# G, U and the turned state in a chunked state recurrence on one Trainium2 core: two column halves on TensorE, all copies on ScalarE

## The chip, the cores and the metric

The kernel runs on one core of one Trainium2 chip. The metric is the device time of one execution in microseconds. Before the change it was timed three times: the median is 735.41 us (730.02 to 738.67). Five engines work side by side, each through its own queue in program order: TensorE (PE, with its weight loads shown apart as PEld), VectorE (DVE), ScalarE (ACT), GpSimd (POOL) and SyncE (SP), which issues the DMAs.

## The reference

The inputs are r, k, v, w, a, b of shape 4 x 8 x 768 x 40 (32 heads, 768 steps, 40 features). A recurrence over the steps makes the output of each head, and a small mixture of four attention experts then reads it:

```
for t in range(S):
    y[:, :, t] = np.einsum('bhd,bhde->bhe', rt, state)
    Sa = np.einsum('bhde,bhe->bhd', state, at)
    state_decay = state * wt[:, :, None, :] - np.einsum('bhd,bhe->bhde', Sa, bt)
    state = state_decay + np.einsum('bhd,bhe->bhde', vt, kt)
...
for e in range(E):
    scores = scale * (q @ k.transpose(0, 2, 1))      # causal
    ye = softmax(scores) @ v @ wo[e]
    out += gate of the top 2 of 4 experts * ye
```

The change touches the recurrence alone.

## The kernel before, in words

The 768 steps are cut into 24 chunks of 32 steps (index c), and four chunks make one of six rounds (w). The 32 heads are cut into four groups of eight (g). A **unit** u = 4c + g is one chunk for eight heads, so there are 96 units, and 16 of them make a round. For a unit the kernel runs seven short stages, each a burst of TensorE products into PSUM with a copy behind it:

- s_k (L358) transposes keys and b's; two ScalarE copies (L365) put them into LS.
- s_g (L366) makes G: for each of eight heads one product with 33 stationary columns and 40 moving columns (L371) into one PSUM tile `ps`, then one ScalarE copy of 32 x 320 (L372) into GT.
- s_u (L373) makes U from G by the inverted triangle in TT (L377), then one ScalarE copy of 32 x 320 with the sign turned (L378) into R2.
- s_v (L379) transposes V and U (L383), copied by ScalarE (L384) into VU.
- s_f (L385) makes the masked products (L388); VectorE applies the mask (L389).
- s_y (L390) makes the outputs and the new state (L396) from LS and R2. Even heads go to PSUM partitions 0 to 39 and odd heads to 64 to 103, by `tile_position=(0, 64 * s)`. ScalarE copies the state out (L406), or VectorE scales it in the last chunk of a round (L404). The function that s_y returns (`decay`, L408) has VectorE scale the outputs.
- s_t (L415) runs for every second unit: it transposes the new state of 16 heads into the PSUM tile `pt` (L420) and copies it, "turned", into the next chunk's LS in two pieces of 40 x 320. For g = 0 the copies are ScalarE's (L427), for g = 2 VectorE's (L425).

A loop over iterations n writes the stages of different units in the fixed order of the table MAIN (L433): u of unit n-1, g of unit n, y of unit n-3, f of unit n-2, t of unit n-6 (n even), a k now and then, and v of unit n-1. So y at iteration n+1 needs the turned state that t copied at iteration n.

Between the stages the table SIDE (L30; SIDE1 and SIDE2 for the first rounds) places the preparation of later rounds by iteration and by slot, a slot being the place behind the stage of that number in MAIN. Preparation means scans over the decays (L267, L273), products with them (L276, L281) and mask copies (L290) on VectorE, 16 matmuls at a time (L289) on TensorE, flags (L264) and copies (L283) on ScalarE. The inversion of the next round's triangles is a chain of two-operation steps (L319, L321) split between POOL and VectorE; its result goes through memory by DMA (L323, L326) into TT. Slot 3, which takes most of VectorE's side work, lies between the mask of f (L389, with L408) and the copies of t (L425).

The products of s_k, s_g, s_u, s_v, s_f and L289 share four PSUM buffers `ps` in turn (L151); `py` has two, `pt` one. After the 96 units comes the attention part (from L650), which the change leaves as it was.

Of the kernel before, what the change touches and what calls it, by code (L numbers as in the profile page):

```python
# [8 lines left out]
AF = mybir.ActivationFunctionType  # L9
# [132 lines left out]
def recurrence(tc, ctx, I, xT, FL, CM, early, tail=None, KP=(11, 11, 11, 11, 11, 11)):  # L142
# [5 lines left out]
    V, A, T, PL = nc.vector, nc.scalar, nc.tensor, nc.gpsimd  # L148

    def ps(shape):  # L150
        return pp.tile(shape, F32, name="ps", tag="ps", bufs=4)  # L151
# [41 lines left out]
    hd = lambda t, d: t.rearrange("p (h d) -> p h d", d=d)  # L193
# [156 lines left out]
    def unit(u):  # L350
        c, g = divmod(u, 4)
        w, cw = divmod(c, 4)
        i = w * NG + g
        h0 = 8 * g
        gl, tt, ls, r1, r2, rb, sc = GF[w % 2], TF[w % 2], LS[c % 2], R1[c % 2], R2[c % 2], RB[c % 2], SC[i % 12]
        gt, vu, xt, py = GT[g], VU[u % 2], XT[g // 2][:, 4 * (g % 2):4 * (g % 2) + 4], PY[u % 2]
        rn, ln = R1[(c + 1) % 2], LS[(c + 1) % 2]
        def s_k():  # L358
            p_k = ps([128, 4, 128])
            for p in range(4):  # L360
                T.transpose(p_k[:, p, 0:104], KB[i % NKB][0:104, p * 4 + cw:p * 4 + cw + 2, :].rearrange("q c k -> q (c k)"),  # L361
                            ident[0:104, 0:104])
            p_k = p_k.rearrange("q p (s e) -> q (p s) e", s=2)[:, :, 0:40]
            for k in range(2):
                A.activation((ls, ln)[k][0:64, h0:h0 + 8], p_k[64 * k:64 * k + 64], AF.Copy)  # L365
        def s_g():  # L366
            p_g = ps([33, 8, 40])
            for h in range(8):
                o = 1024 * g + 64 * ((h // 2) * 4 + cw) + 32 * (h % 2)
                r = 104 * ((h0 + h) // 2) + 64 * (h % 2)  # L370
                T.matmul(p_g[:, h], gl[:, o:o + 33], r1[:, r:r + 40], start=True, stop=True)  # L371
            A.activation(gt[32 * g:32 * g + 32], p_g[0:32], AF.Copy)  # L372
        def s_u():  # L373
            p_u = ps([33, 8, 40])
            for h in range(8):
                o = 64 * ((h // 2) * 4 + cw) + 32 * (h % 2)
                T.matmul(p_u[:, h], tt[:, o:o + 33], gt[:, h, :], start=True, stop=True)  # L377
            A.activation(hd(r2[32:64, 40 * h0:40 * h0 + 320], 40), p_u[0:32], AF.Copy, scale=-1.0)  # L378
        def s_v():  # L379
            p_t = ps([80, 4, 66])  # L380
            for p in range(4):
                o = 40 * (h0 + 2 * p)
                T.transpose(p_t[:, p], r2[0:66, o:o + 80], ident[0:66, 0:66])  # L383
            A.activation(vu[0:80], p_t[:, :, 0:64], AF.Copy)  # L384
        def s_f():  # L385
            p_f = ps([64, 8, 32])
            for p in range(4):
                T.matmul(p_f[:, 2 * p:2 * p + 2], vu[:, p, :], rb[:, 4 * g + p, :], start=True, stop=True)  # L388
            V.tensor_tensor(hd(r2[0:64, 1280 + 32 * h0:1536 + 32 * h0], 32), p_f, mask[:, None, :].to_broadcast([64, 8, 32]), op=OP.mult)  # L389
        def s_y():  # L390
            a = r2[:, 0:40]
            for p in range(4):
                for s in range(2):
                    h = h0 + 2 * p + s
                    m = bass.AP(a.tensor, a.offset + 40 * h, [a.ap[0], [1280 - 8 * h, 2], [1, 40]])
                    T.matmul(py[64 * s:64 * s + 40, p], ls[:, h, :], m, start=True, stop=True, tile_position=(0, 64 * s))  # L396
            for s in range(2):
                q = slice(64 * s, 64 * s + 40)
                if c < 23:
                    o = rn[64:104, 52 * h0:52 * h0 + 416].rearrange("q (p e) -> q p e", p=4)[:, :, 64 * s:64 * s + 40]  # L400
                    st = py[q, :, 0]
                    if cw == 3:
                        pn = PC[((c + 1) // 4 * NG + g) % 12]
                        V.tensor_tensor(o, st, pn[q, :, None].to_broadcast([40, 4, 40]), op=OP.mult)  # L404
                    else:
                        A.activation(o, st, AF.Copy)  # L406
            def decay():
                V.tensor_tensor(xt[:, :, 32 * cw:32 * cw + 32], py[0:104, :, 1, 0:32],  # L408
                                sc.rearrange("q (p c) t -> q p c t", p=4)[:, :, cw, 0:32], op=OP.mult)
                if cw == 3:  # L410
                    for s in range(2):
                        nc.sync.dma_start(xT.rearrange("b (p s e) t -> b s e p t", s=2, e=40)[g, s, :, :, 128 * w:128 * w + 128],
                                          xt[64 * s:64 * s + 40])
            return decay
        def s_t():  # L415
            if c == 23:
                return
            for P in range(8):
                o = 52 * h0 + 104 * P
                T.transpose(PT[0:104, P // 4, 104 * (P % 4):104 * (P % 4) + 104], rn[0:104, o:o + 104], ident[0:104, 0:104])  # L420
            for s in range(2):
                o = ln[64:104, h0 + s:h0 + 16:2].rearrange("q (b p) e -> q b p e", b=2)
                x = PT[64 * s:64 * s + 40, :, 0:416].rearrange("q b (p e) -> q b p e", p=4)[:, :, :, 64:104]
                if g:
                    V.tensor_copy(o, x)  # L425
                else:
                    A.activation(o, x, AF.Copy)  # L427
        return dict(k=s_k, g=s_g, u=s_u, v=s_v, f=s_f, y=s_y, t=s_t)


# [80 lines left out]
    for n in range(NU + 4):  # L511
# [4 lines left out]
        for s, (x, d) in enumerate(MAIN):  # L516
            if x == "k":
                g = {7: 0, 1: 1, 3: 2, 5: 3}.get(n % 8)
# [440 lines left out]
```

## Time and profile before

| what | value |
|---|---|
| median of three runs | 735.41 us |
| profiled execution, its own time | 737.55 us |
| its span | 735.5 us |
| PE, PEld busy | 636.8, 563.0 us |
| DVE, ACT, POOL busy | 519.7, 466.6, 333.5 us |
| the units (first L371 to last L396) | 69.7 to 482.9 us |
| matmul instructions of G, U and y in the trace | 1536 each |

Busy time is the time in which an engine has at least one instruction running. For PE it says little on how much faster it could go, because matmuls overlap. "PEclk" is the clock that TensorE was granted, as a share of the full one. A wait is idle time of an engine put down to the instruction whose end released it; idle time of an engine that nobody waits for costs nothing. Each product of a head shows as two matmul instructions, so the eight of a stage are 16.

### The profile page before, as it was taken

To read this page: it belongs to the slowest core of one execution; us is meant where nothing else is said; L and a number is where in the kernel's file an instruction comes from. 1 tells how busy PE (TensorE), PEld (TensorE's weight loads), DVE (VectorE), ACT (ScalarE), POOL (GpSimd) and SP (SyncE) were. 2 spreads that over 40 slices of the span, in tenths; PEclk is the share of its full clock that TensorE was granted. 3 is DMA by queue.
4 is the path that set the end of the run, shared out by engine and by line. 5 is a ranking of instruction groups with operands and counts; after the bars stand their busy time and mean duration, and the time that the engine had idled before them with its cause. 6 is when DMAs were issued, how large, how long until landed. Compare 5 with 4: busy or idle time off the path is not lost.

```text
span 735.5 us, 22110 instructions
## 1 busy us (share of the span) xinstructions
PE 636.8 (87%) x8801; PEld 563.0 (77%) x8801; DVE 519.7 (71%) x1270; ACT 466.6 (63%) x1144; POOL 333.5 (45%) x512
## 2 busy tenths in 40 slices
PE   5531798898899888988899999979989999999996
PEld 4531788897789777987798999978868777887774
DVE  8899879668866876677657435258797687658651
ACT  6695487477657755766566768727656565656752
POOL 5475388139704850486018301013565354433641
PEclk8555799999999989989999999999999999999999
DMA  7851653575357535753452382143123113201101
GB/s 201 201 149 37 133 159 107 121 199 137 97 136 190 129 89 124 199 130 96 112 147 70 96 227 72 34 140 98 44 69 96 36 39 86 62 28 45 37 32 45
DMA packets 88551, 78.13 MB, mean 106 GB/s; under 512 B 54776, under 2 KB 72952, under 8 KB 88440
## 3 DMA queue, kind: packets, MB, share of 16 engines
q1 hardware_dynamic: 88296, 76.54, 39.9%
q8 instruction: 71, 1.16, 0.7%
q14 instruction: 40, 0.33, 0.2%
q10 hardware_dynamic: 144, 0.10, 0.1%
HBM read 56.17 MB, written 14.16 MB: 96 GB/s over the span
## 4 chain that ended last, share of the span: by engine, by line
PE 59%; DVE 22%; ACT 8%; issue 3%; DMA 1%; SPq 0%; POOL 0%; ACTq 0%; DVEq 0%; POOLq 0%
PE py L396 7%; PE ps L377 6%; PE ot L843 5%; PE ps L289 5%; PE ps L371 5%; PE ps L388 5%; PE sc L795 4%; PE pt L420 4%; PE pt L825 3%; PE pt L852 3%; PE pt L717 3%; PE ps L361 3%; PE pt L736 3%; DVE SC L273 2%; DVE MT L321 2%
## 5 line engine op out<-in xcount | busy, mean ns | idle before, releaser
L817 POOL TENSOR_TENSOR P<-P,m 128x128 f32<-128x128 f32 (+2 forms) x96 | 87.6, 934 | 103.1 <-DVE m L813 50.3
L396 PE MATMUL py<-R,LS 128*40 128x80 f32 x1536 | 84.9, 244 | 31.2 <-DVE LS L425 28.8
L289 PE MATMUL ps<-AB,KB 104*64 104x64 f32 x768 | 68.4, 262 | 38.6 <-ACT LS L365 16.1
L321 POOL TENSOR_TENSOR MT<-MT,TP 128x84 f32<-128x84 f32 (+13 forms) x169 | 89.9, 532 | 13.2
L289 PEld LDWEIGHTS ps<-AB,KB 104*64 104x64 f32 x768 | 63.3, 174 | 42.5 <-ACT LS L365 16.3
L389 DVE TENSOR_TENSOR R<-ps,CM 64x256 f32<-64x256 f32 x96 | 39.9, 415 | 78.4 <-PE ps L388 77.3
L396 PEld LDWEIGHTS py<-R,LS 128*40 128x40 f32 x1536 | 63.7, 122 | 36.3 <-DVE LS L425 33.8
L806 ACT ACTIVATE P<-sc,m 128x128 f32<-128x128 f32 (+2 forms) x96 | 60.7, 633 | 30.2 <-DVE m L805 24.5
L805 DVE TENSOR_REDUCE m<-sc 128x1 f32<-128x128 f32 (+2 forms) x96 | 59.4, 622 | 27.9 <-PE sc L798 26.8
L377 PE MATMUL ps<-GT,TT 128*33 128x40 f32 x1536 | 76.1, 207 | 0.0
L406 ACT ACTIVATE R<-py 40x160 f32<-40x160 f32 x144 | 42.5, 295 | 46.0 <-PE py L396 42.3
L377 PEld LDWEIGHTS ps<-GT,TT 128*33 128x33 f32 x1536 | 65.0, 116 | 7.5 <-issue 1.0
L795 PE MATMUL sc<-ks,qs 128*128 128x384 f32 (+4 forms) x256 | 64.4, 353 | 3.9 <-ACT P L806 3.6
L388 PE MATMUL ps<-RB,VU 128*64 128x64 f32 x768 | 63.4, 228 | 2.1 <-ACT VU L384 2.1
L365 ACT ACTIVATE LS<-ps 64x320 f32<-64x320 f32 x96 | 41.4, 431 | 30.6 <-PE ps L361 29.4
L388 PEld LDWEIGHTS ps<-RB,VU 128*64 128x64 f32 x768 | 56.1, 144 | 3.5 <-ACT VU L384 3.5
L825 PE MATMUL pt<-CM,P 128*128 128x128 f32 x336 | 51.9, 276 | 2.1 <-ACT pt L831 1.7
L319 POOL TENSOR_TENSOR TP<-LT,MT 128x220 f32<-128x220 f32 (+9 forms) x100 | 49.7, 497 | 7.8
L384 ACT ACTIVATE VU<-ps 80x256 f32<-80x256 f32 x96 | 36.4, 379 | 26.3 <-PE ps L383 24.5
L372 ACT ACTIVATE GT<-ps 32x320 f32<-32x320 f32 x96 | 40.7, 424 | 14.8 <-PE ps L371 11.4
L795 PEld LDWEIGHTS sc<-ks,qs 128*128 128x128 f32 x256 | 41.3, 191 | 11.2 <-ACT P L806 8.5
L378 ACT ACTIVATE R<-ps 32x320 f32<-32x320 f32 x96 | 40.9, 426 | 7.6 <-PE ps L377 5.6
(148 smaller groups left out, 1498.0 us busy)
## 6 DMA issues: line engine op xcount, KB each, us to landing
RB<-in_RB SPq DMA_DIRECT2D x24, 320.0 KB
EK<-in_EK SPq DMA_DIRECT2D x18, 416.0 KB
ks<-ks SPq DMA_DIRECT2D x32, 192.0 KB
R<-in_VG SPq DMA_DIRECT2D x24, 208.0 KB
EW<-in_EA SPq DMA_DIRECT2D x18, 214.5 KB
R<-in_VT SPq DMA_DIRECT2D x48, 80.0 KB
R<-in_RT SPq DMA_DIRECT2D x24, 160.0 KB
xT<-XT SPq DMA_DIRECT2D x48, 80.0 KB
```

What stands on the lines that cost most here:

```text
L289: T.matmul(p_a[:, p, cc, :], kb[0:104, n, :], AB[0:104, n, :], start=True, stop=True)
L319: return [lambda: e.tensor_tensor(tmp, row[:, None, :].to_broadcast([128, m, n]), M[:, r0:r0 + m, j][:, :, None].to_broadcast([128, m, n]) ...
L321: lambda: e.tensor_tensor(o, o, tmp, op=OP.add)]
L377: T.matmul(p_u[:, h], tt[:, o:o + 33], gt[:, h, :], start=True, stop=True)
L388: T.matmul(p_f[:, 2 * p:2 * p + 2], vu[:, p, :], rb[:, 4 * g + p, :], start=True, stop=True)
L396: T.matmul(py[64 * s:64 * s + 40, p], ls[:, h, :], m, start=True, stop=True, tile_position=(0, 64 * s))
L406: A.activation(o, st, AF.Copy)
L795: T.matmul(ps[:, c, 0:cw], QS[b][:, e, o], KS[b][:, e, z, k], start=(z == 0), stop=(z == 1 and not last), skip_group_check=True)
L805: V.tensor_reduce(m[:, 0, t:t + 1], ps[:, 0:ch, 0:cw], axis=AX.XY, op=OP.max, negate=True)
L806: later(DE, lambda: A.activation(pv, ps[:, 0:ch, 0:cw], AF.Exp, bias=m[:, 0, t:t + 1], accum_out=m[:, 1, t:t + 1]))
L817: PL.tensor_tensor(P[:, 0:n], P[:, 0:n], m[:, 3, t:t + 1].to_broadcast([128, n]), op=OP.mult)
L825: T.transpose(p[:, 128 * y:128 * y + 128], st["P"][t][:, 128 * c:128 * c + 128], ident)
```

## The change

G and U get PSUM tiles of 97 partitions and four columns of heads. The even heads are made in the array's columns from 0 and land on partitions 0 to 32, the odd heads in the columns from 64 and land on partitions 64 to 96, as y's heads already do. Each of the two copies of a unit becomes two pieces of 32 x 160, one for the even heads and one for the odd, and writes every second head. Both pieces of both copies of the turned state are ScalarE's.

```
         def s_g():
-            p_g = ps([33, 8, 40])
+            p_g = ps([97, 4, 40])
             for h in range(8):
-                o = 1024 * g + 64 * ((h // 2) * 4 + cw) + 32 * (h % 2)
-                r = 104 * ((h0 + h) // 2) + 64 * (h % 2)
-                T.matmul(p_g[:, h], gl[:, o:o + 33], r1[:, r:r + 40], start=True, stop=True)
-            A.activation(gt[32 * g:32 * g + 32], p_g[0:32], AF.Copy)
+                p, s = divmod(h, 2)
+                o = 1024 * g + 64 * (p * 4 + cw) + 32 * s
+                r = 104 * (h0 // 2 + p) + 64 * s
+                T.matmul(p_g[64 * s:64 * s + 33, p], gl[:, o:o + 33], r1[:, r:r + 40], start=True, stop=True, tile_position=(0, 64 * s))
+            for s in range(2):
+                A.activation(gt[32 * g:32 * g + 32, s::2], p_g[64 * s:64 * s + 32], AF.Copy)
         def s_u():
-            p_u = ps([33, 8, 40])
+            p_u = ps([97, 4, 40])
             for h in range(8):
-                o = 64 * ((h // 2) * 4 + cw) + 32 * (h % 2)
-                T.matmul(p_u[:, h], tt[:, o:o + 33], gt[:, h, :], start=True, stop=True)
-            A.activation(hd(r2[32:64, 40 * h0:40 * h0 + 320], 40), p_u[0:32], AF.Copy, scale=-1.0)
+                p, s = divmod(h, 2)
+                o = 64 * (p * 4 + cw) + 32 * s
+                T.matmul(p_u[64 * s:64 * s + 33, p], tt[:, o:o + 33], gt[:, h, :], start=True, stop=True, tile_position=(0, 64 * s))
+            for s in range(2):
+                A.activation(hd(r2[32:64, 40 * h0:40 * h0 + 320], 40)[:, s::2], p_u[64 * s:64 * s + 32], AF.Copy, scale=-1.0)
...
-                if g:
-                    V.tensor_copy(o, x)
-                else:
-                    A.activation(o, x, AF.Copy)
+                A.activation(o, x, AF.Copy)
```

The line numbers below the change move: L371 becomes L372, L372 becomes L374, L377 becomes L380, L378 becomes L382, L383 L387, L384 L388, L388 L392, L389 L393, L396 L400, L406 L410, L408 L412, and L425 and L427 both become L428.

VectorE's queue, in an iteration in which a round's side work stands between the mask of f and the turned state, before:

```order
L389 TENSOR_TENSOR R_127<-ps,CM 64x256
L408 TENSOR_TENSOR XT_132<-py_79,SC_94 104x4x32
L321 TENSOR_TENSOR MT_117<-MT_117,TP_119 128x7x13
L319 TENSOR_TENSOR TP_119<-MT_117 128x96
L321 TENSOR_TENSOR MT_117<-MT_117,TP_119 128x8x12
L273 SCALAR_TENSOR_TENSOR SC_99<-EW_83,D1P_86 104x528
L276 TENSOR_TENSOR AB_112<-EA_84,SC_99 40x16x32
L425 COPY LS_123<-pt 40x8x40 x2
L319 TENSOR_TENSOR TP_119<-MT_117 128x99
```

and now:

```order
L393 TENSOR_TENSOR R_127<-ps,CM 64x256
L412 TENSOR_TENSOR XT_132<-py_79,SC_94 104x4x32
L321 TENSOR_TENSOR MT_117<-MT_117,TP_119 128x7x13
L319 TENSOR_TENSOR TP_119<-MT_117 128x96
L321 TENSOR_TENSOR MT_117<-MT_117,TP_119 128x8x12
L273 SCALAR_TENSOR_TENSOR SC_99<-EW_83,D1P_86 104x528
L276 TENSOR_TENSOR AB_112<-EA_84,SC_99 40x16x32
L319 TENSOR_TENSOR TP_119<-MT_117 128x99
```

The pair of copies has left the queue, and nothing else in it has moved: the mask of the next f now follows the side work directly.

ScalarE's queue at such a place, before (an iteration and a half, from a flag on; VU is the copy of v, R_126 and R_127 that of u, GT that of g, py that of y):

```order
L264 ACTIVATE JK,FL<-EW_83,CM 104x512
L384 ACTIVATE VU_128<-ps 80x256
L378 ACTIVATE R_126<-ps 32x320
L372 ACTIVATE GT_134<-ps 32x320
L406 ACTIVATE R_125<-py_79 40x4x40 x2
L384 ACTIVATE VU_129<-ps 80x256
L378 ACTIVATE R_127<-ps 32x320
L372 ACTIVATE GT_135<-ps 32x320
```

and now:

```order
L264 ACTIVATE JK,FL<-EW_83,CM 104x512
L388 ACTIVATE VU_128<-ps 80x256
L382 ACTIVATE R_126<-ps 32x4x40 x2
L374 ACTIVATE GT_134<-ps 32x4x40 x2
L410 ACTIVATE R_125<-py_79 40x4x40 x2
L428 ACTIVATE LS_122<-pt 40x8x40 x2
L388 ACTIVATE VU_129<-ps 80x256
L382 ACTIVATE R_127<-ps 32x4x40 x2
L374 ACTIVATE GT_135<-ps 32x4x40 x2
```

The two copies of the turned state now stand between the copies of y and the copy of v, and the copies of u and g are two instructions each.

TensorE's queue keeps its order, but the other tile shape changes what its instructions wait for. Before:

```order
L361 MATMUL ps<-CM,KB_107 128x104 x3
L383 MATMUL ps<-CM,R_126 80x66 [waits DMAHW3_49,Activation_49]
L383 MATMUL ps<-CM,R_126 80x66 x3
L377 MATMUL ps<-GT_135,TT_120 33x40 [waits Activation_49]
L377 MATMUL ps<-GT_135,TT_120 33x40 x7
L371 MATMUL ps<-R_124,GLe 33x40 [waits DVE_49]
```

and now:

```order
L361 MATMUL ps<-CM,KB_107 128x104 x3
L387 MATMUL ps<-CM,R_126 80x66 [waits DMAHW3_49,PE_49,Activation_49]
L387 MATMUL ps<-CM,R_126 80x66 x3
L380 MATMUL ps<-GT_135,TT_120 33x40 [waits PE_49,Activation_49]
L380 MATMUL ps<-GT_135,TT_120 33x40 x7
L372 MATMUL ps<-R_124,GLe 33x40 [waits DVE_49]
```

Many products now wait for an earlier product of TensorE itself as well, the one that used the same `ps` buffer before. Counted over the whole queue, instructions with more than one wait carry 171 more of these further waits than before (586 against 415).

## Prediction, made before the changed kernel was run

> **What bounds the kernel now.** I read the page first, then the waits between 60 and 484 us (where the units run), then the busy time round by round, and at last the timeline at one of the long waits.
>
> ```profile
> span 735.5 us, 22110 instructions
> PE 636.8 (87%) x8801; PEld 563.0 (77%) x8801; DVE 519.7 (71%) x1270; ACT 466.6 (63%) x1144; POOL 333.5 (45%) x512
> PEclk8555799999999989989999999999999999999999
> PE 59%; DVE 22%; ACT 8%; issue 3%; DMA 1%; SPq 0%; POOL 0%; ACTq 0%; DVEq 0%; POOLq 0%
> ```
>
> TensorE leads with 87%, yet 22% of the chain that ended last is VectorE's. So there are places where PE stands and DVE sets the pace. The waits name them:
>
> ```profile
> engine line waited for: us in total, times, longest us
> PEld py L396 <- DVE LS L425: 33.8, 29, 3.4
> DVE XT L408 <- ACT R L406: 6.4, 13, 0.9
> PE py L396 <- DVE R L389: 2.2, 2, 1.6
> PE ps L388 <- ACT VU L384: 2.1, 8, 0.5
> ```
>
> Nearly all that PE waits for in steady work is one thing: y (L396) waits for VectorE's copies of the turned state, 29 times, 33.8 us. ScalarE's copies of the same kind (L427) release nobody there, and ScalarE as a whole holds PE up for little (2.1 us for VU). One such wait:
>
> ```profile
> 332.35 0.46 DVE L321 TENSOR_TENSOR MT<-MT,TP 128x96 f32<-128x96 f32 x1
> 332.72 0.41 ACT L372 ACTIVATE GT<-ps 32x320 f32<-32x320 f32 x1
> 332.74 1.25 DVE L273 TENSOR_TENSOR_SCAN SC<-EW,D1P 104x528 f32<-104x528 f32 x1
> 334.02 0.77 DVE L276 TENSOR_TENSOR AB<-EA,SC 40x512 f32<-40x512 f32 x1
> 334.82 1.01 DVE L425 COPY LS<-pt 40x320 f32<-40x320 f32 x2
> 335.36 0.33 PE L396 MATMUL py<-R,LS 128*40 128x80 f32 x2 [2.91 <-DVE LS L425]
> 336.67 0.62 ACT L406 ACTIVATE R<-py 40x160 f32<-40x160 f32 x2 [3.54 <-PE py L396]
> ```
>
> DVE works off its side jobs in order and reaches the copies late. ACT has been idle for 3.54 us meanwhile. By rounds of 16 units and the two stages behind them (first the stretch and its length, then the busy times in the header's order, then the granted clock):
>
> ```profile
> core 0: us, PE busy (x) PEld busy (x) DVE busy (x) ACT busy (x) POOL busy (x), PEclk, DMA share, GB/s
> 81.40:152.60 71.20, 63.60 (x1147) 59.17 (x1146) 54.91 (x118) 47.33 (x121) 36.22 (x63) 0.93 0.51 126
> 152.60:225.10 72.50, 63.97 (x1185) 59.42 (x1184) 56.18 (x124) 47.65 (x121) 37.71 (x64) 0.95 0.56 142
> 225.10:300.20 75.10, 66.54 (x1189) 61.84 (x1188) 55.45 (x123) 47.89 (x121) 36.74 (x64) 0.91 0.53 135
> 300.20:375.30 75.10, 66.78 (x1187) 62.33 (x1186) 52.78 (x120) 46.23 (x117) 37.07 (x64) 0.91 0.49 125
> 375.30:429.00 53.70, 51.88 (x1061) 48.90 (x1059) 30.21 (x85) 37.43 (x97) 25.56 (x61) 1.00 0.46 115
> 429.00:484.00 55.00, 53.11 (x1082) 49.84 (x1080) 21.15 (x57) 38.15 (x97) 3.97 (x12) 1.00 0.35 101
> ```
>
> Rounds 2 to 4 lose twice: PE idles some 8.5 us in each, and the granted clock falls to 0.91-0.95 on average, where it is 1.00 in the two stages without stalls. The last round splits into a heavy stretch of ten iterations and a light one:
>
> ```profile
> 309.60:359.30 49.70, 41.38 (x694) 38.17 (x692) 38.35 (x88) 29.42 (x79) 32.10 (x57) 0.86 0.41 112
> 359.30:378.30 19.00, 19.00 (x366) 18.06 (x363) 10.59 (x23) 12.10 (x27) 0.00 (x0) 1.00 0.59 121
> ```
>
> In the heavy one PE is idle for 8.3 us and runs at 0.86; in the light one it is busy throughout and sets the pace.
>
> **The change part by part: ScalarE and VectorE.**
>
> ```profile
> L425 DVE COPY LS<-pt x46: 483/490/496, 112.4 to 480.2; 40x320 f32<-40x320 f32 x46
> L427 ACT ACTIVATE LS<-pt x46: 428/430/433, 102.8 to 474.7; 40x320 f32<-40x320 f32 x46
> L372 ACT ACTIVATE GT<-ps x96: 411/425/428, 71.0 to 476.0; 32x320 f32<-32x320 f32 x96
> L378 ACT ACTIVATE R<-ps x96: 426/426/429, 82.9 to 477.8; 32x320 f32<-32x320 f32 x96
> L406 ACT ACTIVATE R<-py 40x160 f32<-40x160 f32 x144 | 42.5, 295 | 46.0 <-PE py L396 42.3
> ```
>
> DVE loses 46 x 0.49 = 22.5 us. ACT gains 46 x 0.43 = 19.8 us. A piece of 32 x 160 has the free size of L406's 295 ns, so two take 0.59 where one took 0.425: 0.165 us more, 192 times, 31.7 us. ACT goes from 466.6 to about 518 us, all of it before 484 us. Per unit it is 0.33 us, plus 0.86 for each pair of turned copies that moves. ACT has room for it: in the rounds it goes from some 47 to 47 + 5.3 + 4 = 56 of 75 us. Where that cover is gone, the 51.5 us lie on the path in part; that is the third rival.
>
> **TensorE.** The trace shows no product of 40 columns in halves. The nearest rows are of the undisturbed stage, at full clock:
>
> ```profile
> 413.06 0.69 PE ps L377 x16
> 413.75 0.54 PE ps L371 x15
> 414.29 0.59 PE py L396 x16
> 414.88 0.47 PE ps L388 x8
> ```
>
> An instruction with 40 columns in one half (L371) takes 0.54/15 = 36 ns and one with 64 columns (L388) 59 ns: 0.9 ns a column. L396 has 80 columns, but alternates between the two halves, and takes 0.59/16 = 37 ns: 0.46 a column, so the halves do overlap. If 40 columns follow that, a stage of 16 falls from 0.57 to 0.29 us. If 37 ns is instead what an instruction with its weight load needs, nothing is gained. Per unit (two stages) that is 0 to 0.57 us; lacking a row between, I take the middle, 0.28, or 27 us of PE time in 96 units. It counts only where PE sets the pace.
>
> The Trainium skill, page "TensorEngine Tiling (Array Packing)", section "Performance Considerations", speaks against this: each matmul has about 60 cycles of overhead, and no tiling factor should be taken from a dimension that is already small; 40 is below 60. By that G and U would stay as they are. The rows above differ in part, as 40 columns cost less than 64 in proportion.
>
> **The added waits.** TensorE has 171 further waits on itself, for products several bursts back, so they are met when reached. A further wait is an instruction of its own:
>
> ```profile
> L371 PEldq EVENT_SEMAPHORE  x43: 51/51/1749, 64.4 to 471.0; - x43
> ```
>
> At 51 ns that is 8.7 us if none is hidden by running ahead, 0 if all are. Such waits stand in L371's queue today and no wait row is put down to them, so I take nearer the lower end, 2.5. Behind a waiting one stands all of PE's queue.
>
> **The sum.** In the heavy stretch PE's work at full clock is 41.38 less the 0.14 x 49.7 = 7.0 that the half clock cost, 34.4 us, and 10 x 0.28 less in halves: 31.6. DVE's is 38.35 - 6 x 0.49 = 35.4. ACT's is 29.42 + 10 x 0.33 + 6 x 0.43 = 35.3. y no longer waits for side jobs that stand behind the mask of its own unit; DVE then has about an iteration to work them off. The floor is 35.4. In 375-429 us the span is 3.5% above the busiest engine, but there one engine leads alone; with three side by side I take 15%, 41 us, 8.7 less than now. The ends are 36.6 (3.5%) and 46.8 (only the copies' own 2.9 go). The other six iterations of a round gain 6 x 0.28 = 1.7 on a full PE (0 to 3.4). That is 10 a round; round 2 has less half clock, so 29 for rounds 2 to 4 (9 to 48). Round 1 idles partly for its start and has few of these copies: 5 (0 to 10). In 375-429 PE could give 1.8 idle and 16 x 0.28 = 4.5; I take 3.5 (-2 to 9). In 429-484 PE falls to 48.6 and ACT rises to 38.15 + 5.3 + 4.3 = 47.7, so they hinder each other: 2 (-4 to 6). After 484 us nothing changes. Together 29 + 5 + 3.5 + 2 - 2.5 = 37 us off the profiled execution's 737.55: 700.5. The median of the runs lies 2.1 below that execution: **698 us**.
>
> **The rivals.** First, the halves give nothing on short products (the skill's rule above): without 0.28 a unit the six light iterations and the last two stages gain about 10 less, and 709 follows. For it: 36 and 37 ns an instruction look alike. Against it: the cost per column. 12%.
>
> Second, VectorE stays the bound: y waits for the mask (L389) in the place of L425, since DVE has 35.4 us in the heavy stretch anyway. Then only 2.9 go there, three rounds give 3 x 4.4 = 13, round 1 gives 2, the rest 3: 18 off, 717. For it: DVE's 38.35 of 49.70 us with bursts. Against it: only 2.2 us of such waits today. 14%.
>
> Third, ScalarE becomes the bound and the time rises. The turned copies queue behind y's, u's and g's pieces, and now y waits for ACT at all 46 unit pairs and not at 29, at today's mean 33.8/29 = 1.17 us: 46 x 1.17 = 53.8 for 33.8, 20 us more; less some 8 of the halves it is 12 slower, 748. It decides from the point where ACT's work in an iteration passes PE's. For it: 47.7 against 48.6 in the last stage, and L408 of DVE already waits 13 times for L406. Against it: ACT's idle 3.54 us just where y waits. 8%. The same page of the Trainium skill, under "PSUM Bottleneck", advises both ScalarE and VectorE for emptying PSUM once tiling speeds up TensorE; the change does the opposite. ACT's 63% does not yet bear that out.
>
> Fourth, the three engines interlock well and the heavy stretches take 36.6 us: three rounds give 3 x (13.1 + 1.7) = 44, round 1 gives 8, the last stages 6 and 4; less 2.5 that is 59.5 off, 676. For it: all three have under 36 us of work there. Against it: bursts of 3 us (L273, L276, L425 above) have to even out within an iteration. 9%.
>
> **How the numbers follow.** The forecast has 57%. A measurement can tell about 1% (7 us) from no change. The range 674 to 722 leaves out the third rival and the outer edges of the second and the fourth. Faster by over 1% takes the forecast, the first, most of the second and the fourth: 0.86. Within 1%: 0.07, slower: 0.07.
>
> **What would show it.** Right: no wait of y for DVE's turned copies, waits of y below 12 us in all, PEclk near 1.00 in the rounds, L380 and L372 at 0.36-0.50 us for 16, pieces at 295 ns, rounds 2 to 4 at 62-66 us. Wrong: y waiting for L428 (ACT) or L393 (DVE) for more than 15 us, ACT busy above 90% in a round, or rounds above 70 us.

## The result, and the profile after

The changed kernel takes 697.9 us (median of 4 runs, 695.64 to 699.67); the kernel before, with one more run beside it, 736.95 us. The ratio is 0.9485, with a 95% interval of 0.9415 to 0.9555. The forecast was 698 us, range 674 to 722. The profiled execution took 697.25 us, its span is 695.5 us.

The page of the changed kernel, the lines that answer to those shown of before:

```profile
PE 591.6 (85%) x8801; PEld 503.5 (72%) x8801; DVE 498.6 (72%) x1224; ACT 521.2 (75%) x1382; POOL 338.2 (49%) x512
PEclk8555589999999999999999999999999999999998
PE 47%; DVE 20%; ACT 18%; issue 5%; DMA 4%; SPq 0%; POOL 0%; DVEq 0%; ACTq 0%; POOLq 0%
```

TensorE has lost 45 us of busy time (636.8 before), VectorE 21, and ScalarE has gained 55. The chain that ended last tells more than the sums: ScalarE's share of it has gone from 8% to 18% and TensorE's from 59% to 47%, while VectorE's is nearly what it was. The waits between 60 and 484 us, as far as y and the next buffers are concerned:

```profile
DVE XT L412 <- ACT R L410: 29.7, 42, 1.6
PEld ps L392 <- ACT VU L388: 12.5, 26, 1.3
PEld py L400 <- ACT LS L428: 9.7, 27, 0.8
PEld ps L372 <- ACT LS L365: 9.2, 9, 1.2
PEld ps L372 <- ACT R L410: 3.9, 11, 0.8
PEld ps L380 <- ACT GT L374: 3.2, 10, 0.4
PEld py L400 <- DVE R L393: 1.9, 2, 1.2
```

No row has y waiting for a turned copy of VectorE's any more; there were 33.8 us of it, the longest 3.4. In their place stand many short waits, and of the rows shown all but the last name ScalarE. The costs of the pieces and what TensorE's weight loads of y sat idle for, from the groups by line and form (busy us, mean ns of one, then the idle time before):

```profile
L400 PEld LDWEIGHTS py<-R,LS 128*40 128x40 f32 x1536 | 63.0, 119 | 15.0 <-ACT LS L428 9.7 <-DVE R L393 1.9 <-ACT VU L388 1.0
L382 ACT ACTIVATE R<-ps 32x160 f32<-32x160 f32 x192 | 56.7, 295 | 4.5 <-PE ps L380 1.2
L374 ACT ACTIVATE GT<-ps 32x160 f32<-32x160 f32 x192 | 56.5, 295 | 12.4 <-PE ps L372 8.6
```

The rounds of 16 units and the stage behind them, cut at the same units as in the prediction (stretch and length, busy times of PE, PEld, DVE, ACT and POOL, granted clock):

```profile
81.20:148.10 66.90, 57.39 (x1149) 50.90 (x1147) 53.09 (x115) 54.83 (x157) 36.38 (x63) 0.93 0.54 132
148.10:211.70 63.60, 56.90 (x1184) 50.10 (x1182) 52.74 (x114) 57.59 (x163) 39.91 (x64) 0.97 0.61 160
211.70:275.70 64.00, 55.78 (x1188) 50.00 (x1187) 49.74 (x114) 57.05 (x161) 38.49 (x64) 0.97 0.65 161
275.70:339.40 63.70, 56.05 (x1188) 49.83 (x1186) 48.53 (x110) 55.69 (x158) 40.02 (x64) 0.97 0.61 152
339.40:389.00 49.60, 46.93 (x1063) 41.29 (x1060) 28.42 (x79) 45.80 (x136) 25.37 (x61) 1.00 0.43 114
```

They were 71.2, 72.5, 75.1, 75.1 and 53.7 us. The changes are -4.3, -8.9, -11.1, -11.4 and -4.1 us. For the last 15 units before the tail (from the 81st product U to the 96th) the same row of before, and then of after:

```profile
429.60:477.40 47.80, 47.61 (x988) 45.11 (x986) 18.02 (x47) 36.91 (x95) 3.97 (x12) 1.00 0.36 106
```

```profile
389.60:438.20 48.60, 45.55 (x980) 38.75 (x974) 15.17 (x40) 45.43 (x132) 3.99 (x12) 1.00 0.41 111
```

This stage has become 0.8 us longer, although TensorE has 2 us less to do in it. All together that is 39.0 of the 40.3 us between the two profiled executions. A second profile of the changed kernel (from its run once more, below) has the same two last stretches, 49.6 and 48.6 us, but rounds of 69.1, 64.0, 64.3 and 65.2 us: a difference of a microsecond or two in one round can't be told from chance, one in the last stretches can.

### The profile page after: what moved, and what is told of

It is laid out like the page before. It is cut to its first block, busy times and chain, and to the rows that moved or that the text cites. A ratio compares the mean times of both kernels' runs of the same rounds, so it can differ in the third digit from the quotient of the medians.

```text
span 695.5 us, 22403 instructions
## 1 busy us (share of the span) xinstructions
PE 591.6 (85%) x8801; PEld 503.5 (72%) x8801; DVE 498.6 (72%) x1224; ACT 521.2 (75%) x1382; POOL 338.2 (49%) x512
## 3 DMA queue, kind: packets, MB, share of 16 engines
q1 hardware_dynamic: 88296, 76.54, 42.8%
## 4 chain that ended last, share of the span: by engine, by line
PE 47%; DVE 20%; ACT 18%; issue 5%; DMA 4%; SPq 0%; POOL 0%; DVEq 0%; ACTq 0%; POOLq 0%
PE ot L844 5%; PE py L400 5%; PE sc L796 4%; PE ps L289 4%; PE ps L392 4%; PE pt L826 4%; PE pt L853 4%; PE pt L718 3%; DVE MT L321 3%; ACT R L382 3%; ACT GT L374 3%; PE pt L424 3%; ACT LS L428 3%; ACT LS L365 3%; PE ps L380 3%
## 5 line engine op out<-in xcount | busy, mean ns | idle before, releaser
L289 PE MATMUL ps<-AB,KB 104*64 104x64 f32 x768 | 64.5, 252 | 42.8 <-ACT LS L365 18.3
L289 PEld LDWEIGHTS ps<-AB,KB 104*64 104x64 f32 x768 | 59.1, 164 | 46.9 <-ACT LS L365 18.9
L400 PE MATMUL py<-R,LS 128*40 128x80 f32 x1536 | 83.6, 238 | 7.7 <-ACT LS L428 2.5
L807 ACT ACTIVATE P<-sc,m 128x128 f32<-128x128 f32 (+2 forms) x96 | 60.8, 634 | 31.2 <-DVE m L806 25.4
L400 PEld LDWEIGHTS py<-R,LS 128*40 128x40 f32 x1536 | 63.0, 119 | 15.0 <-ACT LS L428 9.7
L393 DVE TENSOR_TENSOR R<-ps,CM 64x256 f32<-64x256 f32 x96 | 39.6, 412 | 44.7 <-PE ps L392 43.8
L392 PE MATMUL ps<-RB,VU 128*64 128x64 f32 x768 | 63.9, 228 | 7.9 <-ACT VU L388 7.2
L374 ACT ACTIVATE GT<-ps 32x160 f32<-32x160 f32 x192 | 56.5, 295 | 12.4 <-PE ps L372 8.6
L392 PEld LDWEIGHTS ps<-RB,VU 128*64 128x64 f32 x768 | 54.4, 142 | 12.8 <-ACT VU L388 12.5
L382 ACT ACTIVATE R<-ps 32x160 f32<-32x160 f32 x192 | 56.7, 295 | 4.5 <-PE ps L380 1.2
L319 POOL TENSOR_TENSOR TP<-LT,MT 128x220 f32<-128x220 f32 (+9 forms) x100 | 52.6, 526 | 7.8
L826 PE MATMUL pt<-CM,P 128*128 128x128 f32 x336 | 51.9, 276 | 2.0 <-ACT pt L832 1.7
L380 PE MATMUL ps<-GT,TT 128*33 128x40 f32 x1536 | 50.0, 207 | 2.6 <-ACT GT L374 1.6
L412 DVE TENSOR_TENSOR XT<-py,SC 104x128 f32<-104x128 f32 x96 | 27.1, 282 | 32.1 <-ACT R L410 29.7
L796 PEld LDWEIGHTS sc<-ks,qs 128*128 128x128 f32 x256 | 40.8, 189 | 11.7 <-ACT P L807 9.0
L428 ACT ACTIVATE LS<-pt 40x320 f32<-40x320 f32 x92 | 39.7, 431 | 10.6 <-PE pt L424 8.4
L832 ACT ACTIVATE pt<-pt 128x512 f32<-128x512 f32 (+1 forms) x64 | 34.4, 542 | 17.5 <-PE pt L826 16.6
L365 ACT ACTIVATE LS<-ps 64x320 f32<-64x320 f32 x96 | 41.5, 433 | 7.4 <-PE ps L361 5.8
```

The source lines that it names most:

```text
L289: T.matmul(p_a[:, p, cc, :], kb[0:104, n, :], AB[0:104, n, :], start=True, stop=True)
L374: A.activation(gt[32 * g:32 * g + 32, s::2], p_g[64 * s:64 * s + 32], AF.Copy)
L380: T.matmul(p_u[64 * s:64 * s + 33, p], tt[:, o:o + 33], gt[:, h, :], start=True, stop=True, tile_position=(0, 64 * s))
L382: A.activation(hd(r2[32:64, 40 * h0:40 * h0 + 320], 40)[:, s::2], p_u[64 * s:64 * s + 32], AF.Copy, scale=-1.0)
L796: T.matmul(ps[:, c, 0:cw], QS[b][:, e, o], KS[b][:, e, z, k], start=(z == 0), stop=(z == 1 and not last), skip_group_check=True)
L807: later(DE, lambda: A.activation(pv, ps[:, 0:ch, 0:cw], AF.Exp, bias=m[:, 0, t:t + 1], accum_out=m[:, 1, t:t + 1]))
```

## The experiments

The theory after the result: two things happened. The turned copies left VectorE's queue, which ended the long waits of y; and G and U in halves took time off TensorE, of which only a part came through, since their split copies load ScalarE (the runs bear the last part out for the last stages, and not for the rounds). The rivals: the halves carry more than that, or VectorE or the transfers set the pace of what is left. Line numbers differ a little between the kernels; the names stay.

### The turned copies alone

The kernel before, with only this edit of the change:

```diff
-                if g:
-                    V.tensor_copy(o, x)
-                else:
-                    A.activation(o, x, AF.Copy)
+                A.activation(o, x, AF.Copy)
```

> Only the turned state's copies move to ScalarE; G and U stay in one half with one copy each. My theory (the stall of y behind VectorE's side work carries the gain): rounds 2 to 4 fall from 72.5-75.1 us to 66-68, PEclk there to about 0.97, the two last stages stay at 53-55 us; in all 24 to 30 us off, 707 to 713 us. Rival (the column halves carry the gain, and y would wait for the mask L389 in the place of the copies): rounds stay at 71 us or more, 722 us or more.

Measured: 702.97 us, ratio 0.9546 [0.9479, 0.9612]. This is 33 of some 38 us, and more than expected. The intervals of this kernel and of the changed one overlap, but none of its four runs (700.59 to 706.6) is as fast as the slowest of the changed kernel's ten (694.85 to 700.2, with the six of its run once more). The rounds are 66.9, 66.4, 65.6, 64.5 and 51.1 us, the last 15 units 47.8.

### The halves alone

The changed kernel, with this edit undone:

```diff
-                A.activation(o, x, AF.Copy)
+                if g:
+                    V.tensor_copy(o, x)
+                else:
+                    A.activation(o, x, AF.Copy)
```

> Only G and U in halves with their copies in two pieces; the turned state of g = 2 stays VectorE's. My theory: y still waits for VectorE's copies, as long as before or longer (30 to 40 us), rounds 2 to 4 stay at 69 to 73 us; but the two last stages, where VectorE is idle more than half the time, fall to 47-50 us each, since ScalarE then has 43 us of work in them and not 46-48; in all 14 to 24 us off, 713 to 723 us. Rival (the halves carry the gain): rounds at 66 us or less, 705 us or less.

Measured: 738.07 us, ratio 1.0034 [1.0000, 1.0069]. Neither number was met: the halves alone give nothing, although TensorE is busy for 608.7 us in the place of 636.8. The waits of this kernel say where the time went:

```profile
PEld py L400 <- DVE LS L429: 49.7, 37, 4.6
PE py L400 <- DVE LS L429: 42.6, 27, 4.5
```

TensorE reaches y earlier, and waits there so much longer for VectorE: 49.7 us where the kernel before had 33.8.

### Where the halves gain and where they lose

A round consists of a heavy stretch of ten units (from the 4th product U of a round to the 14th), in which VectorE's side jobs lie, and a light one of six behind it. Cut there, the third and the fourth round read as follows (heavy, light, heavy, light), first before, then with the turned copies alone, then the changed kernel:

```profile
234.70:284.30 49.60, 41.04 (x693) 37.68 (x693) 38.75 (x87) 29.28 (x79) 32.46 (x58) 0.86 0.43 118
284.30:309.70 25.40, 25.40 (x496) 24.07 (x493) 16.32 (x36) 18.50 (x43) 5.06 (x8) 1.00 0.77 175
309.70:359.40 49.70, 41.38 (x694) 38.25 (x693) 38.25 (x88) 29.42 (x79) 32.01 (x57) 0.86 0.41 111
359.40:384.80 25.40, 25.40 (x496) 24.08 (x494) 12.81 (x31) 16.88 (x39) 2.19 (x8) 1.00 0.63 149
```

```profile
224.10:264.30 40.20, 35.21 (x694) 32.78 (x693) 35.78 (x82) 33.32 (x87) 35.50 (x62) 1.00 0.52 141
264.30:289.70 25.40, 25.40 (x496) 24.07 (x495) 14.98 (x34) 18.08 (x42) 5.89 (x8) 1.00 0.80 193
289.70:328.80 39.10, 35.10 (x694) 32.78 (x694) 35.96 (x81) 32.66 (x86) 34.68 (x58) 1.00 0.49 132
328.80:354.10 25.30, 25.30 (x495) 23.99 (x492) 11.72 (x29) 17.00 (x39) 1.57 (x7) 1.00 0.65 158
```

```profile
220.00:261.50 41.50, 33.28 (x692) 29.18 (x691) 34.78 (x82) 36.81 (x108) 34.82 (x62) 0.96 0.56 148
261.50:284.00 22.50, 22.50 (x500) 20.82 (x497) 14.96 (x33) 20.24 (x54) 4.22 (x3) 1.00 0.86 193
284.00:325.30 41.30, 33.68 (x693) 29.14 (x692) 35.62 (x81) 37.18 (x109) 36.11 (x62) 0.96 0.52 136
325.30:347.50 22.20, 22.17 (x492) 20.68 (x492) 12.32 (x29) 18.16 (x49) 0.95 (x5) 1.00 0.74 180
```

In the light stretches TensorE is busy from end to end in all three, and the halves take them from 25.4 to 22.5 and 22.2 us: (25.4 - 22.5) / 6 = 0.48 and 3.2 / 6 = 0.53 us a unit. In the heavy ones the turned copies take 49.6 to 40.2 and 49.7 to 39.1; with the halves added, the time goes up again, to 41.5 and 41.3. There TensorE has 1.4 to 1.9 us less to do and ScalarE 3.5 to 4.5 us more (33.32 to 36.81, 32.66 to 37.18). But TensorE's granted clock is lower there too, 0.96 for 1.00: (1 - 0.96) x 41.5 = 1.7 us by the prediction's own reckoning of the half clock, about as much as the stretches lost (1.3 and 2.2). The waits don't name this rival. The chain through the two heavy stretches of the changed kernel (220.0 to 261.5 and 284.0 to 325.3 us), and through the first with the turned copies alone (224.1 to 264.3), by line:

```profile
by line: ACT LS L365 11.5%; issue 10.7%; PE py L400 9.2%; ACT R L410 9.2%; ACT R L382 8.5%; ACT LS L428 8.4%; ACT GT L374 8.3%; PE ps L392 6.5%; ACT JK L264 5.9%; PE ps L289 4.3%; ACT VU L388 3.9%; PE pt L424 3.5%; PE ps L372 3.3%; PE ps L3
```

```profile
by line: DMA EK<-in_EK 17.1%; DMA LT<-Ld 12.6%; DVE TP L319 9.4%; DVE MT L321 8.8%; DVE KB L281 7.1%; issue 6.2%; DVE SC L273 6.1%; DVE AB L276 4.6%; PE pt L424 3.8%; ACT JK L264 3.7%; PE ps L392 3.6%; DVE R L393 3.4%; DVE SUF L267 2.8%; DV
```

```profile
by line: DMA R<-in_RT 13.0%; DVE MT L321 10.6%; DVE TP L319 9.8%; DVE KB L281 6.5%; DVE SC L273 6.0%; issue 5.7%; PE ps L371 4.9%; DVE AB L276 4.5%; PE py L396 4.4%; PE pt L420 4.3%; DVE R L389 4.0%; ACT LS L365 3.9%; PE ps L388 3.5%; DVE S
```

With the turned copies alone the chain runs through VectorE's side jobs. With the halves it runs through ScalarE in the first stretch, where seven lines of it hold 56%, but through transfers and VectorE's side jobs in the second, which is just as long. So the chain doesn't say that ScalarE is what makes the heavy stretches longer; the next kernels test it.

### One copy in the place of two, and a split without halves

The first kernel is the changed one with one copy of 32 x 320 that reads the even half twice, so that the odd heads' G and U are left out (their products are still made); the second makes G and U in one half, but copies them in two pieces.

```diff
-            for s in range(2):
-                A.activation(gt[32 * g:32 * g + 32, s::2], p_g[64 * s:64 * s + 32], AF.Copy)
+            A.activation(gt[32 * g:32 * g + 32].rearrange("q (p s) e -> q p s e", s=2),
+                         p_g[0:32, :, None, :].to_broadcast([32, 4, 2, 40]), AF.Copy)
```

> The changed kernel, but G and U are copied by one instruction of 32 x 320 that reads the even heads' half twice; the odd heads' G and U are left out (the even ones stand in their place). ScalarE loses the split's 31.7 us, all else stays. If ScalarE is now the bound (my theory), the last two stages fall from 49.6 and 55.0 us to 45-48 and 49-51, rounds by 2 to 3 us, in all 12 to 20 us: 678 to 686 us. Rival (TensorE or VectorE bounds it, ScalarE's time is hidden): 694 us or more.

```diff
-            A.activation(gt[32 * g:32 * g + 32], p_g[0:32], AF.Copy)
+            for s in range(2):
+                A.activation(gt[32 * g:32 * g + 32, s::2], p_g[0:32, s::2], AF.Copy)
```

> Both turned copies are ScalarE's, G and U are made in one half as in the kernel before, but each is copied in two pieces (even heads, odd heads). Two kernels with the halves stand at 698 us (copies split) and 688 us (one copy), and one without them at 703 us (one copy); this one is the fourth corner. My theory: splitting costs ScalarE 0.33 us a unit and this falls on the path above all where ScalarE is nearly as busy as TensorE, so some 7 to 12 us are added here too: 710 to 715 us, the last stage above 48.5 us. Rival: the split costs nothing by itself and the 10 us came from something else that the one-copy kernel left out: 700 to 705 us.

Measured: 687.94 us, ratio 0.9332 [0.9259, 0.9405], 2 us above what my theory said; and 703.52 us, ratio 0.9562 [0.9524, 0.9600]. So with the halves the split costs 10 us (697.9 to 687.9), and without them nothing that can be told (702.97 to 703.52): here the second one's number is its rival's, and my 710 to 715 was wrong. The last 15 units, of the kernel with one copy and of the one with a split but no halves:

```profile
383.80:428.00 44.20, 42.67 (x995) 37.62 (x991) 15.05 (x40) 38.93 (x100) 3.97 (x12) 1.00 0.40 117
```

```profile
395.10:443.20 48.10, 48.01 (x990) 45.14 (x989) 14.80 (x40) 41.20 (x132) 3.98 (x12) 1.00 0.37 105
```

Without halves TensorE fills the stage and covers the pieces (48.01 of 48.10 us). With the halves and one copy the stage falls to 44.2, and with halves and two pieces it is 48.6, with 45.4 us of ScalarE in it. The two costs are not quite the same, though: a pair of pieces takes less in the kernel without halves. First that one, then the changed kernel, on the timeline:

```profile
421.76 0.48 ACT L380 ACTIVATE R<-ps 32x160 f32<-32x160 f32 x2
```

```profile
420.61 0.60 ACT L382 ACTIVATE R<-ps 32x160 f32<-32x160 f32 x2
```

So the split adds 10 us to ScalarE's busy time where there are no halves (485.9 to 496.0 us by the pages) and 37 where there are (484.6 to 521.2). That it would be free without halves at this full price as well was not shown. In the rounds the one copy gave nothing that can be told: 62.4, 64.9 and 62.9 us for 63.6, 64.0 and 63.7. Its heavy stretches, beside the 41.5 and 41.3 of the changed kernel:

```profile
216.40:259.20 42.80, 34.79 (x696) 31.20 (x694) 34.78 (x81) 33.04 (x88) 35.15 (x62) 0.88 0.53 145
281.40:322.00 40.60, 33.09 (x693) 29.98 (x694) 34.78 (x82) 32.76 (x87) 34.50 (x62) 0.92 0.53 144
```

ScalarE has some 4 us less to do there than in the changed kernel, and together the two stretches are no shorter; but the granted clock is lower still. Here are the four kernels side by side, all with the turned copies on ScalarE; two numbers are those of the third and the fourth round (stretches in us):

| kernel | light | heavy | clock in the heavy ones | stage before the last | last 15 units |
|---|---|---|---|---|---|
| one half, one copy | 25.4, 25.3 | 40.2, 39.1 | 1.00, 1.00 | 51.1 | 47.8 |
| one half, two pieces | 25.3, 25.4 | 39.9, 39.6 | 1.00, 1.00 | 51.1 | 48.1 |
| two halves, one copy | 22.2, 22.2 | 42.8, 40.6 | 0.88, 0.92 | 47.4 | 44.2 |
| two halves, two pieces (changed) | 22.5, 22.2 | 41.5, 41.3 | 0.96, 0.96 | 49.6 | 48.6 |

The price of the split lies in the two last columns: 2.2 and 4.4 of the 8.1 us between the two profiled executions (697.25 and 689.19). The heavy stretches are longer with the halves whether the copies are split or not, and the clock is lower in each of these four. Whether they are longer because of the clock, because of the added waits of TensorE on itself or for another reason was not tested. ScalarE's pieces are not shown to be it, nor are they ruled out: by the same reckoning the clock may cost the kernel with one copy 0.12 x 42.8 = 5.1 and 0.08 x 40.6 = 3.2 us, and hide a gain.

### Where ScalarE's order sets the pace

The timeline of the changed kernel in the last stage shows how this works:

```profile
409.58 0.89 ACT L428 ACTIVATE LS<-pt 40x320 f32<-40x320 f32 x2
410.49 0.38 ACT L388 ACTIVATE VU<-ps 80x256 f32<-80x256 f32 x1
410.52 0.50 PEld L400 LDWEIGHTS py<-R,LS 128*40 128x40 f32 x13 [0.30 <-ACT LS L428]
410.90 0.60 ACT L382 ACTIVATE R<-ps 32x160 f32<-32x160 f32 x2
411.52 0.60 ACT L374 ACTIVATE GT<-ps 32x160 f32<-32x160 f32 x2
412.15 0.61 ACT L410 ACTIVATE R<-py 40x160 f32<-40x160 f32 x2
412.27 0.48 PE L380 MATMUL ps<-GT,TT 128*33 128x40 f32 x16
412.78 0.88 ACT L365 ACTIVATE LS<-ps 64x320 f32<-64x320 f32 x2
413.71 0.48 PE L372 MATMUL ps<-R,GL 128*33 128x40 f32 x16 [0.95 <-ACT LS L365]
```

ScalarE works without a gap from 409.58 to 413.66 us, in the program's order. The next G (L372) needs one of the four buffers ps, which come free in the same order, and the last of ScalarE's copies ahead of it is L365's. Each piece that is put into this queue moves all that stands behind it. Two kernels took work out of it in the last two stages: the turned copies of the second pair from chunk 16 on back to VectorE, or the odd heads' pieces of G and U from chunk 16 on.

```diff
-                A.activation(o, x, AF.Copy)
+                if g and c >= 16:
+                    V.tensor_copy(o, x)
+                else:
+                    A.activation(o, x, AF.Copy)
```

> The changed kernel, but from chunk 16 on (the two last stages) the turned copies of g = 2 are VectorE's again, where VectorE is busy for 28.4 of 49.6 and 16.8 of 55.0 us. If ScalarE bounds these stages, 6 and 10 pieces of 0.43 us leave its path: the last stage falls by 3 to 6 us, the one before by 0 to 3, in all 690 to 695 us. Rival (the y's wait for VectorE comes back there): no gain or a loss, 697 us or more.

```diff
-                A.activation(gt[32 * g:32 * g + 32, s::2], p_g[64 * s:64 * s + 32], AF.Copy)
+                if s and c >= 16:
+                    V.tensor_copy(gt[32 * g:32 * g + 32, s::2], p_g[64:96])
+                else:
+                    A.activation(gt[32 * g:32 * g + 32, s::2], p_g[64 * s:64 * s + 32], AF.Copy)
```

(and U's likewise, with its factor of -1)

> The changed kernel, but from chunk 16 on the odd heads' pieces of G and of U are copied by VectorE, which is busy 28.4 us and 16.8 us of the last two stages of 49 and 55 us. My theory: in these stages ScalarE hands TensorE its buffers, so taking 0.59 us of 3 us a unit from it shortens the last stage from 48.6 to about 45 us and the one ahead of it by 1 to 2 us; the rounds of 64 us stay: 690 to 694 us. Rival: what counts is the chain of hand-overs and not how busy ScalarE is, and a VectorE that has its own jobs in order hands the buffers back later: 697 us or more.

Measured: 696.46 us, ratio 0.9468 [0.9408, 0.9528], no difference from the changed kernel that can be told, between theory and rival; and 691.74 us, ratio 0.9404 [0.9350, 0.9458], inside what was expected. With the turned copies back on VectorE the last 15 units take 47.4 us, 1.2 less, but the stage before takes 51.9 for 49.6, and in these two stages this wait is back, as the rival said:

```profile
PEld py L400 <- DVE LS L429: 5.1, 10, 1.7
```

The second kernel was run once more, beside the changed kernel on the same chip:

> The changed kernel itself once more, beside the next one on the same chip: 696 to 699 us.

> The kernel of the run e6_vector_odd_late once more (odd heads' pieces of G and U on VectorE from chunk 16 on), beside the changed kernel on the same chip. If it is faster, by what its last stage shows (43.1 for 48.6 us): 5 to 7 us below it, 690 to 693 us. Rival: its gain was between runs, and it stands within 2 us of the changed kernel.

Measured: 699.07 us, ratio 0.9464 [0.9431, 0.9497], for the changed kernel and 691.86 us, ratio 0.9386 [0.9360, 0.9412], for the other. That is 7.2 us and the intervals do not meet. The last 15 units of the other, in this second run:

```profile
391.40:434.50 43.10, 41.65 (x987) 37.10 (x988) 22.94 (x70) 35.98 (x102) 3.97 (x12) 1.00 0.45 129
```

43.1 us for 48.6, as in its first run, with ScalarE at 36.0 for 45.4. This version is faster than the kernel before and the changed one.

### What holds the rounds now

Four kernels asked this. The first two leave out VectorE's part of the inversion in windows 1 to 5, once in the changed kernel and once in the kernel before. The third does so together with the one copy. The fourth leaves out the later loads of EW, EA and EK.

```diff
             if w:
                 tp += step(PL, j, 0, kp, TP[0])
-                td += step(V, j, kp, 32, TP[1])
```

> The changed kernel without VectorE's part of the inversion in windows 1 to 5 (some 38 instructions and 14 us of its 50 us busy in each round are left out; GpSimd's part, the loads and the stores stay). Theory A, VectorE's side work sets the pace of the rounds: they fall from 64 to 58 to 60 us, where TensorE (56 us busy) and ScalarE (57 us) are next, and the time to 680 to 685 us. Theory B, ScalarE and TensorE hand each other the buffers and set the pace: the rounds stay at 62 to 64 us and the time above 692 us.

> The kernel before (turned copies of every second pair on VectorE, G and U in one half, one copy each), without VectorE's part of the inversion in windows 1 to 5 (some 14 us of its work in each round are left out). My theory: before, y waited for the turned copies only because they stood behind side jobs in VectorE's queue; with a third of these gone the waits of y for L425 fall from 33.8 us to under 12 and the rounds from 72 to 75 us to 65 to 67, so most of what moving the copies gave comes without moving them: 700 to 712 us. Rival: the copies cost because of their own length and of the hand-over from TensorE to VectorE and back, whatever else VectorE has to do: rounds 70 or more, 722 us or more.

> The changed kernel with one copy of G and of U in the place of two (the even half is read twice, so that the odd heads' G and U are left out) and without VectorE's part of the inversion in windows 1 to 5. Each relief alone gave the rounds little (from 64 to 62 to 65 us, and to 61 to 63). My theory: in a round VectorE and ScalarE stand beside TensorE in turn, so each relief alone shows the other engine and the two together give more than their sum: rounds of 57 to 59 us, where TensorE (55 to 56 us busy) is left alone, and 668 to 676 us in all. Rival: something else, such as the loads or TensorE's own order, holds the rounds at 61 us: 678 us or more (687.9 less the 4.4 us of the last stage less some 2 of the one before).

```diff
-        if i < 24:
+        if i < 9:
             t = (E8[i] if i < 8 else own)[k]
```

> The changed kernel without the loads of EW, EA and EK for pieces 9 to 23 (840 KB each; the later pieces use the data of piece 8 again, so windows 2 to 5 are computed from wrong decays). It asks whether the transfers hold the rounds of the changed kernel, in whose chain stands a stretch of 17 us of transfers (Ld, LT, EK) at one place. Theory A, the loads are a bound of the rounds beside ScalarE and VectorE: the third and fourth round fall from 64 to 60 to 61 us and the time to 688 to 691 us. Theory B, the chain only passes through them because they are as late as the rest: the rounds stay at 62.5 to 64 us and the time at 694 to 698 us.

In the order of these expectations: 689.08 us, ratio 0.9350 [0.9312, 0.9388]; 715.98 us, ratio 0.9693 [0.9620, 0.9766]; 679.07 us, ratio 0.9213 [0.9146, 0.9280]; and 699.78 us, ratio 0.9492 [0.9457, 0.9527].

Without the late loads nothing is gained (theory B there; the time is even 2 us above its range). Without VectorE's part of the inversion VectorE has 11 to 12 us less to do in a round (53.1 to 41.9 in the first, 52.7 to 40.3 in the second; the 14 of the expectation was too much). The changed kernel's rounds 2 to 4 fall to 61.1, 60.8 and 62.7 us: between theory A and B. The heavy and the light stretch of its third round:

```profile
216.80:255.20 38.40, 33.42 (x693) 28.27 (x694) 24.34 (x44) 36.08 (x107) 33.33 (x59) 1.00 0.54 152
255.20:277.60 22.40, 22.40 (x496) 20.71 (x494) 14.62 (x32) 20.93 (x55) 4.74 (x6) 1.00 0.78 168
```

Of this heavy stretch ScalarE now fills 36.1 of 38.4 us; the one of the fourth round takes 40.3, at a clock of 0.96. So VectorE's side work is worth 1 to 3 us of a heavy stretch, the 3 with the clock back at 1.00. Whether ScalarE stands right behind it is not shown: with both relieved the two stretches take 37.4 and 40.8 us, at a clock of 0.95 and 0.92. Rounds 2 to 4 are then 61.1, 59.7 and 63.0 us, and the time is 3 us above what I expected (679.07 for 668 to 676): the rival's number. The heavy stretch of 37.4 us has 32.4 of TensorE, 31.9 of ScalarE and 23.9 of VectorE in it, and none of these fills it. What sets its pace stays open; transfers of the next chunk (R from RT, 13.0%) stand in one of the chains above, and were not taken away alone.

The kernel before without VectorE's part of the inversion came between its two theories as well: rounds of 72.7, 68.0 and 67.8 us and this wait:

```profile
PEld py L395 <- DVE LS L424: 24.8, 25, 2.8
```

24.8 us of y waiting for the turned copies, where there were 33.8. So thinning the queue ahead of the copies ends a part of the stall, and moving them ends all of it. How much of the rest is due to the side jobs that are left, and how much to VectorE as the place, was not separated.

## Why the prediction was right, and where it was not

**The stall** went as forecast. The turned copies of VectorE release nothing any more, VectorE loses 21.1 us (22.5 forecast), ScalarE gains 54.6 (51.5), the pieces take 295 ns. The heavy stretch was forecast at 41 us from a floor of 35.4 and 15% for three engines side by side; it takes 41.5 and 41.3. But the busiest engine in it is ScalarE (36.8, 37.2) and not VectorE, whose 35.4 was the floor. y waits for 15.0 us in all, above the 12 named as a sign of being right; the clock is 0.97, not quite 1.00; and one sign of being wrong came, if barely: ScalarE is busy for 57.59 of 63.60 us in round 2, 90.6%. By stage the sum holds: 31.4 us for 29 in rounds 2 to 4, 4.3 for 5 in round 1, 4.1 for 3.5 in the stage before the last. Only the last stage went the other way.

**The halves** were mis-sized: the term of 0.28 us a unit is 0.48 to 0.53 where TensorE sets the pace, near the upper bound of 0 to 0.57. The six light iterations gain 2.6 to 3.2 us a round in the place of 1.7. The alternating halves do overlap as L396's row suggested: sixteen instructions of U take 0.48 us on the timeline above, for 0.69 before. The Trainium skill, page "TensorEngine Tiling (Array Packing)", section "Performance Considerations", gives each matmul about 60 cycles of overhead and advises against tiling a dimension that is already small. The prediction took this to leave short products as they were; the light stretches do not bear that reading out, by 3 us in 25.4.

**The net of the halves** was wrong the other way. The first rival put the kernel without them at 709, 11 us above the forecast; the turned copies alone give 703, and the halves another 5. The step that failed is the one that let ScalarE's pieces lie beside other work nearly for nothing: they cost 10 us. In the last stage (2 us gain forecast, 0.8 lost) TensorE's saving is handed back as waits for ScalarE: with one copy the stage takes 44.2 us, with the odd pieces on VectorE 43.1. In the heavy stretches the saving does not come through either, but there one copy in the place of two shortens nothing, at a lower clock, and the cause stays open. The turned copies were worth 33 us and not 26 (37 less the 11). These two errors cancel: that the total of 698 us was met to the microsecond is luck.

**The added waits** of TensorE on itself (2.5 us, 0 to 8.7) were not measured alone. They stand in the light stretches too, and the 0.48 to 0.53 us a unit is what is left after them. In the heavy ones they may be a part of what makes the halves longer; no run shows their price.

**The rivals.** The second (y waits for VectorE's mask) fell: 1.9 us. The third (ScalarE becomes the bound) did not make the kernel slower, but its mechanism is there in the last stages, where the pieces cost most of their 10 us. Here the same page's section "PSUM Bottleneck" of the Trainium skill, which advises ScalarE and VectorE together for emptying PSUM after tiling, is borne out: the odd pieces on VectorE in the late stages gain 7.2 us. Which copies are shared matters: the turned ones on VectorE there gained nothing that can be told. The fourth rival's 36.6 us for a heavy stretch was reached nowhere in rounds 2 to 4; the best is 37.4, with part of the work left out.

## What to carry to other kernels

A saving on one engine is worth what the stage lets through: cut the trace at places where one engine leads alone and where several do, and price an edit in each. In the last stage here ScalarE, which works in order and hands out the buffers, set the pace at 45.4 busy of 48.6 us, before its share looked full. When a product is made in pieces, ask first who copies them out, and split the copies between engines where the second one has room. A chain through one stretch may name another engine than the chain through the next: take work off the engine that it names before calling it the cause.

## What had not been expected

Two copies of 32 x 160 that ScalarE does back to back take 0.48 us when both read the same partitions of a buffer, and 0.60 when the second one reads the other half (rows above): the halves charge the copies by 0.12 us a pair. On the trace the second piece starts 201 ns after the first in the one case, and 305 ns in the other. Whether the partitions or the layout of the source make the difference was not tried. The two copies of y (L410) read every second block of 40 columns, from different partitions, and take 0.61 us, which speaks for the partitions.
